# A new order for the operations of a fused attention and MLP kernel

## The chip, the cores and the metric

The kernel runs on one NeuronCore of a Trainium2 chip. The core has five engines that work side by side, each through its own list of instructions and strictly in the order of that list: TensorE (PE, matrix products and the weight loads that precede them), VectorE (DVE), ScalarE (ACT), GpSimd (POOL) and SyncE (SP, which here only issues transfers). An engine that has reached an instruction whose operand is not ready stands still until a semaphore tells it that the operand is there; everything behind that instruction on the same engine stands still too. Transfers between the off-chip memory and the on-chip memory (SBUF) are issued from the lists of SP, ACT and POOL.

The metric is the device time of one launch in microseconds (us). Before the change three runs took 209.41, 209.46 and 210.68 us; the median is 209.46.

## The reference

The reference is attention with a sliding window and a few always visible "sink" keys, followed by a two-layer MLP whose activation is the square of a ReLU:

```python
scores = scale * q @ k.T                      # 4 batches, 8 heads, 768 positions, head width 64
keep = (key < 4) | (0 <= query - key < 128)   # 4 sink keys, a window of 128
a = softmax(where(keep, scores, -1e9))
x = (a @ v), heads side by side               # 3072 tokens x 512
out = relu(x @ w_in) ** 2 @ w_out             # 512 -> 2048 -> 512, float32 out
```

## The kernel before, in words

**Attention.** A batch is 768 tokens: six tiles of 128, taken in three pairs s = 0, 1, 2. For each pair the kernel forms the scores of two heads at a time (the tile `ps`, line 613), turns them into exponentials on ACT (`expm`, line 634), zeroes what lies outside the window (the "mask": on DVE by a product with a triangle of ones, line 646 or 643, or on POOL by two "selects" of line 218), multiplies by the values (`po`, line 682) with a column of ones that gives the softmax's denominator, and divides on DVE (lines 698 and 699, tile `xn`). The result is turned round to put features on partitions: for batches 0 and 1 by PE (`px`, line 731) with a copy out of PSUM, for batches 2 and 3 by transposing transfers issued from SP (line 713, tile `xT`). Queries and keys need the same turning: in the first tiles of batch 0 they arrive in float32 (`qr`), are cast to bf16 (`qs`, the function `regroup`), turned by PE (`pt`, line 507) and copied out of PSUM (`qkT`, the function `unload`); for batches 2 and 3 this too is done by transposing transfers (line 461).

**The MLP.** Layer 1 of batch 0 and of a part of batch 1 is a plain product (`pm`, line 763), then a ReLU and a square. The rest of layer 1 (line 894) and most of layer 2 (line 1233) use Strassen's scheme: seven products in place of eight, paid for by sums and differences on DVE. The sums on DVE are `xs` (line 852, differences of blocks of `xT`), `sg` and a part of `gT` (line 1207, of blocks of the activations), `wi` (lines 810 and 818) and `wt` (line 1025, of blocks of the weights), all of them with two bf16 operands in SBUF; and `t` (line 936) and `r` (line 963), which read PSUM.

**What sets the order.** The function that builds the kernel makes 946 numbered operations, each with the operations it must follow and the memory rooms it takes. An operation is a handful of instructions: the cast of one block, the eight products of one Strassen term, one issue of a transfer. `Plan.run` then emits them one after the other in the order of the string `ORDER`, which is the whole schedule written out by hand or by a search. A word of it is a number, with up to two additions. A letter chooses the engine where an operation can run on several (`55d`: on DVE, `55a`: on ACT, `g`: on POOL). `+0` or `+1` chooses one of two PSUM pools. Rooms of a pool are given out in turn, first freed first used, so that the order also decides which buffer an operation writes and whom it therefore has to wait for:

```python
for s in o.takes:
    if len(s.pools) > 1:
        s.pool = s.pools[int(chosen.pop(0))]
    s.room = free[s.pool].pop(0)
```

Since each engine runs its own list, the order of the string matters in three ways: the order of instructions on each engine, the order of the transfers on the three issuing queues, and the assignment of rooms.

`DUMMIES` gives some operations a number of idle matmuls that are put ahead of their work on PE, to keep the array busy: 29 in operation 945 (`warmup`, line 1363), 8 in 58, 10 in 63, 4 in 64, 3 each in 83, 91 and 97 (line 185).

Operations that the prediction names, all of batch 0: 8 to 15 are the eight transfers of `qr`, in this order on SP; 55, 56, 61, 62, 67, 68, 73, 74 the casts of what they bring; 57, 58, 63, 64, 69, 70, 75, 76 the turns of these on PE; 59, 60, 65, 66, 71, 72, 77, 78 the copies of the turned blocks out of PSUM; 83, 84, 91, 92 the scores of the first pair of tiles, 85, 86, 93, 94 their exponentials on ACT, 87, 89, 95, 97 their products with the values; 103, 104, 113, 114 the scores of the second pair of tiles, 105, 107, 115, 117 their exponentials and 106, 108, 116, 118 their masks; 99 and 101 the turns of the result and 100 and 102 their copies; 156 is the first layer-1 product, with the first quarter of `w_in`, which operation 21 loads. 79 is the preparation of the sink values on POOL.

Of the kernel before, what the change touches and what calls it, by code (L numbers as in the profile page):

```python
# [18 lines left out]


ORDER = """
944 0 1 2 7 8 9 10 11 12 13 14 15 16 17 18 945+0 3 5 19 20 21 6 79 22 23 24 25 55d 56d 57+0 58 59d 60a 83+0 85 103+1
105 26 27 28 62d 61d 63+1 64 67d 68d 65a 69+0 70 71d 72d 66a 84+1 73a 74a 75+1 76 78d 91+0 86 77a 93 80 113+1 87+0
92+1 89 94 95+0 97 115 88 90 96 98 114+1 99+0 101 117 100d 104+0 81+1 102d 107 82 4 29 106g 30 31 32 33 34 35 36 37 38
39 40 41 42 43 44 45 46 127 47 48 49 50 116d 118d 108d 156+0 109+1 119+1 121 111 162+0 110 120 122 112 123+1 125 124d
126d 157a 163a 158a 164a 168+1 165+0 51 52 53 54 177+0 169a 170d 208g 166a 167a 178d 171+1 179a 172a 128+1 131+0 174+0
173a 132a 129d 319 323 321 175d 324 176d 322 130a 320 159+1 133a 160a 161a 278+0 279 136+1 144+0 145+0 280 281 148 138
146 289+1 149d 139d 274 147d 275 282 290 283 291 292 284 276 277 134+1 137+0 135 286a 140 141d 285 287d 293 150+0 151
294 142+1 196+0 192+1 295 143 193 200+1 198a 202a 195d 197 199d 201 203d 297d 194d 296 298a 152+1 154 204+0 205
212+0+1 153a 155d 189+0 215 206a 213 190a 214 207d 186+0 216 191d 248+0 187d 249d 251+1 209 253a 188d 252a 180+1 181d  # L30
250d 182d 183+0 326 184a 185d 300 301 230+0+1 233 299 288 219+0+1 231 220 304+0 210+0 306a 211 222 305 237+0+0 240
232d 325 302 221 303 223 241d 238 239d 311 307 217+1 254+0 224+0 308a 255 309 218 242+0 225 243 452g 422 423 424 425
426 427 428 429 430 431 432 433 434 234g 235+1 226+0 228 310a 227a 229a 314 236 244+0 246 316a 247a 327 313 245d 329
256+0+1 257 315 328 332 317 330 347+1 333+1 348 334 259 335a 337 312 336 331 338 349a 263+1+1 266 264 339 351 340 341a
350 352 435 436 437 258g 438 439 267g 265g 361+0 353 362 354 363d 260g 364 343 365 366 445 440 453 444 441 355a 356a
342a 448 446 449 442 447 443 451 450 318 344 345 357 375+0 358 376 261+0 359 377a 346a 367 368 379 378 262 380 268+0
270+0 381 382 360a 369a 271a 269 370d 371 272 273d 372 383a 389 373 463+0+0 385 386 466 464 390 408+0 409 394+1 395
410a 391 393 387 411 396a 397 412 456+1+0 413 392 414 398 400 415 374d 388a 457 384a 399 504 458 506 465 467 505 508+0
416a 401 418 419 510a 511 402a 654 655 684g 656 657 658 659 660 661 662 663 664 665 672 459 420 460 685 512a 417a 421a
403a 404 468+0 509 405 513 454+1 469 406 507 514a 455 515 461+0 472+1+0 407a 517 523 542 462 518 519 521 544 675 673  # L40
470 473 546+0 475 543 548a 479+0+0 516 520d 549 480 482 550a 524 481d 545 476d 525 483d 547 495+1+0 551 553 496 552a
498 556 674 676 666 667 668 474g 669 670 499g 471 522 679 488+0+0 555 554 526 497d 484+1 557 491 489 671 492g 490g
477+0 500+0 485 478 559 501 561 527+0 528 529d 563 562 493+0 565 558d 494 534 530 535 531d 566+0 567 532 533a 568d 569
564 570 572 571 536 683 682 677 678 486 502 680 711+0+0 487 503 573 574d 537 538 539d 540 681 541 560 714 712 704+0+0
580+0 581 576 577 582d 583 594 584 585 575a 705 707 688+0+0 713g 715g 706g 708g 689 691 578 586 587 626+1 627 588a
628a 612+0 686+0 613 687 630 596 692 690 595 629 631 716+0 717 589a 614a 632 633 579a 634a 635a 615 590 616 597 617
693+0 694 591 618 636 619 637 592 598+1 599 620a 600a 638 593a 601 622 640+0 641 602 623 642a 736 643 603 644 604 646
605 645 709+0 647 624 740+0 639a 621a 606a 648a 742a 649a 607a 608 609 738 737 650 651 743 739 710 610 611d 741
695+0+0 744a 625a 696 698 652 653d 755 697 699 756 757 745 747 746a 749 748 720+0+0 723 759+0 750 700+0 701 761a 762
751 721 752a 763a 760 722g 753 724g 727+0+1 774 775 758 728 730 725+0 766 764 778+1 779 765a 729d 767 776 726 777 768  # L50
731g 732+1 733 718 719 702 703 754 734 735 793 794 785 770 769 798+1 812+0 799 813 780a 771a 800a 814a 781 782a 797
796 786 772 795 815 801 802 816 817 818 803 783 819 784d 787 820a 804 805 789 822 823 829 826 827 828 791 806a 807a
821a 808 809 788 830+0 831 790a 832a 824 825d 810 858+1 811a 834 872+0 844+1 860a 846a 874a 833 835 836 837 873 845
859 876 838a 839a 886 887 888 875 877 861 840 841 848 862 864 792 773 842 863 847 889 849 878 879 890+0 865 843a 880a
850 882 883 851 892a 881a 866d 867d 884 893 894d 868 869 852a 853a 854 855 870 856 895 891 897 896a 885a 900 857d 871d
905 909+1 899 907 901 924 926 906 898 925 903 911a 912 913a 902a 928+1 904 914 910 929 931+1 915d 908 927 918 920 919
930a 933a 916 922 921d 934 917 923 932 935 936 939 937 938 943 940 942 941
"""
DUMMIES = {
    945: 29, 58: 8, 63: 10, 64: 4, 83: 3, 91: 3, 97: 3,  # L60
# [1340 lines left out]
```

## Time and profile before

| | |
|---|---|
| timed runs | 209.41, 209.46, 210.68 us |
| the profiled execution, first to last instruction (span) | 208.3 us |
| TensorE's granted clock, mean over the span | 1.000 |
| PE busy | 200.5 us (96%), 2476 matmuls |
| weight loads busy | 174.3 us (84%) |
| DVE busy | 173.1 us (83%), 318 instructions |
| ACT busy | 135.9 us (65%), 189 instructions |
| POOL busy | 96.4 us (46%), 138 instructions |
| DMA moved | 26.1 MB |

The page gives the span of the profiled execution, 208.3 us; its own time beyond that is not listed, so what lies around the span is taken from the median of the timed runs: 209.46 - 208.3 = 1.16 us. Rows of a timeline read: start in us from the beginning of the span, length in us, engine, line, operation, what is written and read, size, count, and in brackets the idle time of that engine just before and who ended it. Line numbers are those of the kernel before; the changed kernel's are lower by one from the end of `ORDER` on, since the new string is one line shorter.

### The profile page before, as it was taken

What the parts mean: (1) busy time and instruction counts of PE and PEld (TensorE: products, weight loads), DVE (VectorE), ACT (ScalarE), POOL (GpSimd) and SP (SyncE); (2) the same over time, 40 slices, a digit from 0 to 9 for tenths busy, and PEclk for the clock granted to TensorE, in tenths of its full rate; (3) what the DMA queues carried; (4) which work ended last, traced back from release to release, by engine and by line L of the source; (5) the groups of instructions that cost most, each with busy time, mean ns of one, the idle gap of its engine ahead of it and who ended that gap; (6) DMA issues with size and microseconds to landing.
All of it is one profiled execution on the core that took longest, in us unless ns stands there. A gap on an engine that the chain in (4) does not pass through costs nothing.

```text
span 208.3 us, 5924 instructions
## 1 busy us (share of the span) xinstructions
PE 200.5 (96%) x2476; PEld 174.3 (84%) x2476; DVE 173.1 (83%) x318; ACT 135.9 (65%) x189; POOL 96.4 (46%) x138
## 2 busy tenths in 40 slices
PE   7989999999998999999999998999999999999993
PEld 7658997457986889989878987999888999998893
DVE  6759268867599998999999987999989598999933
ACT  2695888433749589999987047988856248693110
POOL 7999274599599976689356209000043000000000
PEclk9999999999999999999999999999999999999999
DMA  6999999999999999999999945300204203200115
GB/s 190 260 184 207 173 196 215 166 146 142 261 68 148 131 172 137 181 162 121 154 116 220 109 96 134 148 3 0 50 14 145 50 5 113 88 3 0 50 54 201
DMA packets 93994, 26.10 MB, mean 125 GB/s; under 512 B 86800, under 2 KB 91408, under 8 KB 93968
## 3 DMA queue, kind: packets, MB, share of 16 engines
q0 software_dynamic: 69248, 12.59, 80.2%
q1 hardware_dynamic: 24536, 13.01, 27.9%
q8 instruction: 19, 0.31, 0.6%
q10 hardware_dynamic: 184, 0.14, 0.2%
q14 instruction: 7, 0.06, 0.1%
HBM read 27.30 MB, written 6.29 MB: 161 GB/s over the span
## 4 chain that ended last, share of the span: by engine, by line
PE 82%; DVE 5%; DMA 4%; SPq 3%; ACT 2%; issue 2%; DVEq 0%; ACTq 0%
PE py L1233 26%; PE pm L894 23%; PE pm L763 10%; PE py L984 7%; PE po L682 6%; PE ps L613 4%; DMA qr<-in_q_dram 3%; PE pt L507 2%; PE py L1094 2%; SPq L351 2%; DVE t L936 1%; PE px L731 1%; DMA xT<-xn_sb 1%; SPq L461 1%; ACT expm L634 1%
## 5 line engine op out<-in xcount | busy, mean ns | idle before, releaser
L634 ACT ACTIVATE expm<-ps 128x1024 bf16<-128x1024 f32 (+1 forms) x48 | 43.7, 953 | 7.7 <-PE ps L613 7.5
L218 POOL TENSOR_SCALAR_AFFINE_SELECT expm<-expm 128x512 bf16<-128x512 bf16 x34 | 22.7, 705 | 44.2 <-ACT expm L634 40.4
L894 PEld LDWEIGHTS <-w_in_sb 128*128 128x128 bf16 x384 | 32.2, 114 | 2.0 <-issue 1.9
L1233 PEld LDWEIGHTS <-gT_sb 128*128 128x128 bf16 x288 | 27.2, 98 | 4.7 <-issue 1.4
L917 ACT ACTIVATE gT_sb<-r 128x1024 bf16<-128x1024 bf16 x28 | 28.8, 1054 | 2.5 <-DVE r L963 2.3
L894 PE MATMUL pm<-xs,wi 128*128 128x256 bf16 (+1 forms) x288 | 29.2, 246 | 0.1
L192 ACT ACTIVATE osb<-py 128x256 f32<-128x256 f32 (+1 forms) x30 | 11.9, 399 | 25.0 <-PE py L1233 19.8
L936 DVE TENSOR_TENSOR t<-t,pm 128x512 f32<-128x512 f32 x36 | 23.8, 683 | 3.7 <-PE pm L894 2.9
L894 PEld LDWEIGHTS <-wi 128*128 128x128 bf16 x288 | 24.6, 114 | 1.0 <-DVE xs L852 0.4
L1233 PEld LDWEIGHTS <-sg 128*128 128x128 bf16 x216 | 20.3, 98 | 2.7 <-issue 0.5
L963 DVE CUSTOM_DVE_ANT_1 r<-pm,t 128x1024 bf16<-128x1024 f32 x18 | 21.8, 1218 | 0.5 <-PE pm L894 0.5
L763 PE MATMUL pm<-xT,w_in_sb 128*128 128x256 bf16 x192 | 22.0, 273 | 0.0
L763 PEld LDWEIGHTS <-w_in_sb 128*128 128x128 bf16 x192 | 20.6, 114 | 0.3 <-issue 0.2
L894 PE MATMUL pm<-xs,w_in_sb 128*128 128x256 bf16 (+1 forms) x192 | 19.9, 246 | 1.0 <-DVE t L936 1.0
L951 ACT ACTIVATE r<-pm 128x1024 bf16<-128x1024 f32 x16 | 16.3, 1022 | 4.9 <-DVE osb L194 2.3
L1233 PE MATMUL py<-w_out_sb,gT_sb 128*128 128x256 bf16 x144 | 18.7, 273 | 0.6 <-ACT expm L634 0.6
L1233 PE MATMUL py<-wt,sg 128*128 128x256 bf16 x144 | 18.7, 273 | 0.0
L1233 PE MATMUL py<-wt,gT_sb 128*128 128x256 bf16 x144 | 18.5, 273 | 0.0
L682 PEld LDWEIGHTS <-expm 128*128 128x128 bf16 x352 | 16.6, 97 | 1.9 <-issue 0.6
L682 PE MATMUL po<-v,expm 128*128 128x65 bf16 x352 | 17.8, 193 | 0.3 <-ACT expm L634 0.3
L699 DVE TENSOR_TENSOR xn_sb<-po,rc 128x512 bf16<-128x512 f32 (+1 forms) x28 | 17.2, 615 | 1.0
L984 PE MATMUL py<-w_out_sb,gT_sb 128*128 128x512 bf16 x64 | 14.8, 379 | 0.0
(104 smaller groups left out, 376.9 us busy)
## 6 DMA issues: line engine op xcount, KB each, us to landing
out_dram<-osb SPq DMA_DIRECT2D x11, 512.0 KB, 3.7
v<-in_v_dram POOLq DMA_DIRECT2D x24, 128.0 KB, 6.2
qn<-in_k_dram POOLq DMA_DIRECT2D x20, 128.0 KB, 6.1
qn<-in_q_dram POOLq DMA_DIRECT2D x20, 128.0 KB, 6.5
w_in_sb<-in_moe_w_in_dram POOLq DMA_DIRECT2D x4, 512.0 KB, 9.4
w_out_sb<-in_moe_w_out_dram POOLq DMA_DIRECT2D x4, 512.0 KB, 10.8
qr<-in_k_dram SPq DMA_DIRECT2D x4, 256.0 KB, 5.1
qr<-in_q_dram SPq DMA_DIRECT2D x4, 256.0 KB, 4.8
```

The source lines that it names most:

```text
L218: nc.gpsimd.affine_select(out=e_tile, in_=e_tile, compare_op=ALU.is_ge, fill=fill, base=i - 1, pattern=[[0, n], [1 if i else -1, 128]], ch ...
L634: nc.scalar.activation(out=x[:, :, o:512], in_=bank_t["s", b, s, m][:, :, o:512], func=AF.Exp, scale=scale)
L682: touch(("po", b, s, m0), e, nc.tensor.matmul(pv[:, i, h2, :], lhsT=lhsT, rhs=rhs, start=(n_ == 0), stop=(n_ == len(mms) - 1)), j)
L699: touch(("po", b, s, m0), e, nc.vector.tensor_tensor(out=xn_sb[:, 2 * s:2 * s + 2, 128 * (m0 + j0):128 * (m0 + j0 + nj)].rearrange("p i (j ...
L763: nc.tensor.matmul(pm[:, i, :], lhsT=w_in_sb[:, fb // 4, kb, fb % 4:512:4], rhs=xT[:, c0 // 256:(c0 + cw) // 256, kb, :], start=(kb == 0), ...
L894: touch(tag, e, nc.tensor.matmul(y[:, bk, i, :], lhsT=weights(name, f0 + i, a), rhs=rhs[:, a, :], start=fresh and i == 0 and a == 0, stop= ...
L917: nc.scalar.activation(out=d, in_=x, func=AF.Square)
L936: touch(tag, e, nc.vector.tensor_tensor(out=T["t"], in0=T["t"], in1=T["y"][:, bk], op=ALU.subtract), bk)
L951: touch(tag, e, nc.scalar.activation(out=r, in_=T["y"], func=AF.Relu), 0, 1)
L963: touch(tag, e, nc.vector._custom_dve(TENSOR_ADD_SAT, out=r.rearrange("p b n c -> p b (n c)"), in0=T["y"].rearrange("p b n c -> p b (n c)" ...
L984: touch((b, u), e, nc.tensor.matmul(pm[:, i, :], lhsT=gT_sb[:, fb, 128 * t:128 * t + 128], rhs=w_out_sb[:, fb, :], start=(fb == 0), stop=( ...
L1233: touch((b, u), e, nc.tensor.matmul(region(name), lhsT=x[:, i, :], rhs=w_[:, i, :], start=first and i == 0, stop=i == HB - 1, skip_group_c ...
```

## The change

Only the string `ORDER` changes. The 946 operations, their instructions' shapes, the idle matmuls and all other code stay as they are. The new string was found by a search over orders in a replay that models the times at which DVE's sums and GpSimd's selects collide. Of the operations 65 are given to another engine than before; the counts that come of it:

| operation | before | after |
|---|---|---|
| masks | DVE 27, POOL 17 | DVE 28, POOL 16 |
| casts of `qr` (`regroup`) | DVE 6, ACT 2 | DVE 4, ACT 2, POOL 2 |
| ReLUs of plain layer 1 and Strassen layer 1 (`relu`) | ACT 24, DVE 6 | ACT 25, DVE 5 |
| squares of plain layer 1 | ACT 6, DVE 6 | ACT 9, DVE 3 |
| copies of turned blocks (`unload`) | ACT 12, DVE 12 | ACT 11, DVE 13 |

The first lines of the string, where operations 1 to 200 stand, and its last line:

```diff
-944 0 1 2 7 8 9 10 11 12 13 14 15 16 17 18 945+0 3 5 19 20 21 6 79 22 23 24 25 55d 56d 57+0 58 59d 60a 83+0 85 103+1
-105 26 27 28 62d 61d 63+1 64 67d 68d 65a 69+0 70 71d 72d 66a 84+1 73a 74a 75+1 76 78d 91+0 86 77a 93 80 113+1 87+0
-92+1 89 94 95+0 97 115 88 90 96 98 114+1 99+0 101 117 100d 104+0 81+1 102d 107 82 4 29 106g 30 31 32 33 34 35 36 37 38
-39 40 41 42 43 44 45 46 127 47 48 49 50 116d 118d 108d 156+0 109+1 119+1 121 111 162+0 110 120 122 112 123+1 125 124d
+8 0 944 5 55a 9 10 1 11 12 13 14 15 7 3 6 57+1 56d 19 2 58 59a 61d 20 67 60a 68d 945+0 63+1 21 62a 22 23 103+1 73d 74
+64 69+0 24 25 83+0 4 71 65a 105 66a 84+1 70 26 85 75+1 79 72a 86 91+0 76 87+0 27 77 78 89 28 92+1 90 93 114+1 95+0 29
+88 94 97 117 96 30 31 99+0 113+1 80 98 100 32 16 33 34 35 36 115 101 81+1 104+0 102 37 38 116d 156+0 39 82 106d 107
+119+1 118d 109+0 121 108d 40 41 110 42 122 111 162+1 112 43 123+0 120 124 125 168+1 126a 44 163 169 45 157d 164a 170a
...
-930a 933a 916 922 921d 934 917 923 932 935 936 939 937 938 943 940 942 941
+920 932 935 934 922 936 939 921d 937 938 923 943 940 942 941
```

What the prediction speaks of, engine by engine:

- **PE, start.** Before: 945 (29 idle matmuls), 57, 58, 83, 103, 63, 64, 69, 70, 84, 75, 76, 91, 113, 87, 92, 89, 95, 97, 114, 99, 101, 104, 81, 156. After: 57, 58, 945, 63, 103, 64, 69, 83, 84, 70, 75, 91, 76, 87, 89, 92, 114, 95, 97, 99, 113, 101, 81, 104, 156. The same operations stand ahead of 156.
- **ACT, start.** Before: the transfer 7, then 60, 85, 105, 65, 66, 73, 74, 86, 77, 93, 80, 94. After: 55, the transfer 7, 59, 60, 62, 65, 105, 66, 85, 72, 86, 93, 94, 117, 80.
- **POOL, start.** The loads keep their order among themselves. Two casts (67, which waits for transfer 12, and 74, which waits for transfer 15) now stand between them: 67 ahead of the first quarter of `w_in` (21), 74 ahead of the second (24). The preparation of the sink values (79) moves behind all four quarters of `w_in`. The selects of operation 106 go to DVE.
- **SP, batch 2.** The four transposing transfers of the last two pairs of `xT` (486, 502, 487, 503) stand one behind the other; before, a transposing transfer of batch 3's keys (680) stood between 502 and 487.
- **The end.** The last four product operations on PE (932, 935, 936, 939) and what follows them are in the same order as before, but that 921 and 923 come later.

61 lines of the change are left out of this document (30 added, 31 removed).

## The prediction

> **What bounds the kernel now.** I read the page first: the span, the engines' shares and the chain of work that ended last.
>
> ```profile
> span 208.3 us, 5924 instructions
> PE 200.5 (96%) x2476; PEld 174.3 (84%) x2476; DVE 173.1 (83%) x318; ACT 135.9 (65%) x189; POOL 96.4 (46%) x138
> PE 82%; DVE 5%; DMA 4%; SPq 3%; ACT 2%; issue 2%; DVEq 0%; ACTq 0%
> ```
>
> TensorE is busy for 96% and is 82% of the chain. An order can only win where PE stands still, so I asked next for busy times by stretches, cut where PE's share falls.
>
> ```profile
> 0.00:17.00 17.00, 14.69 (x180) 11.14 (x181) 11.51 (x32) 11.23 (x17) 15.28 (x30) 1.00 1.24 211
> 17.00:60.00 43.00, 43.00 (x459) 34.27 (x458) 29.40 (x51) 25.57 (x35) 29.19 (x40) 1.00 1.72 177
> 60.00:65.00 5.00, 4.02 (x49) 2.99 (x47) 4.88 (x9) 3.97 (x7) 5.00 (x7) 1.00 2.09 133
> 65.00:120.00 55.00, 54.85 (x797) 48.77 (x795) 52.83 (x102) 44.02 (x62) 37.91 (x50) 1.00 1.85 150
> 120.00:130.00 10.00, 9.03 (x138) 7.80 (x136) 7.64 (x13) 6.61 (x8) 4.94 (x8) 1.00 0.49 108
> 130.00:203.00 73.00, 73.00 (x844) 67.69 (x843) 64.86 (x111) 44.53 (x63) 4.08 (x6) 1.00 0.16 53
> 203.00:208.30 5.30, 1.96 (x26) 1.68 (x24) 1.95 (x5) 0.00 (x0) 0.00 (x0) 0.99 0.55 198
> ```
>
> The second column is the stretch's length, the third PE's busy time. From 17 to 203 us PE is idle for 0.00 + 0.98 + 0.15 + 0.97 + 0.00 = 2.1 us. That is all that an order can win in the middle. DVE's 52.83 of 55 us are close to a bound, but the 0.15 us beside it say that PE hardly waits for it. The end (5.3 us) is the last product, its sums and the last store; its order is kept, so I cost it at nothing. What is left is the start, where PE's share is padded by idle matmuls. The chain of waits shows what set it:
>
> ```profile
> 4.48 6.15 DMA qr<-in_q_dram
> ...
> 10.72 0.64 ACT qs L192
> ...
> 13.76 0.82 ACT expm L634
> ...
> 16.62 1.87 PE pm L763 x16
> ```
>
> The last transfer of `qr` (15) lands at 10.63, a cast takes 0.64, the last exponential of the first tiles (94) runs from 13.76 to 14.58, and the first layer-1 product (156) starts at 16.6. From there to 60 us PE never stops. So the time is the start of 156, plus PE's work (the same operations after 156 in both orders), plus PE's waits, plus the end.
>
> **Term 1, the start.** Timelines of PE and ACT:
>
> ```profile
> 1.27 3.28 PE L1363 MATMUL pw<-tri 128*128 128x128 bf16 x29 [1.27 <-DVE tri L224]
> 4.34 0.63 PE L507 MATMUL pt<-ident,qs 128*128 128x128 bf16 x4
> ...
> 5.62 0.63 PE L507 MATMUL pt<-ident,qs 128*128 128x128 bf16 x4
> ...
> 7.48 0.73 PE L185 MATMUL pt<-ident 128*128 128x128 bf16 x10
> 8.19 0.40 PE L507 MATMUL pt<-ident,qs 128*128 128x128 bf16 x4
> ```
>
> ```profile
> 8.08 1.02 ACT L634 ACTIVATE expm<-ps 128x1024 bf16<-128x1024 f32 x1
> 8.98 1.09 ACT L192 ACTIVATE qkT<-pt 128x512 bf16<-128x512 bf16 x2
> 9.94 1.41 ACT L192 ACTIVATE qs<-qr 128x512 bf16<-128x512 f32 x2
> 11.25 0.79 ACT L634 ACTIVATE expm<-ps 128x768 bf16<-128x768 f32 x1
> ```
>
> The 29 idle matmuls take 3.28 us, the last one alone 0.31, so they start (3.28 - 0.31) / 28 = 0.106 us apart. The ten of 7.48 are (0.73 - 0.22) / 9 = 0.057 apart. PE runs at half rate first and at full rate from about 7 us. The old order puts the 29 where PE has nothing to do, before the first cast is ready. The new one puts them behind the first two turns. There: 55's cast (now ACT, 0.64) ends near 4.2, as DVE's did. Turns 57, eight idle matmuls, turns 58 are 16 x 0.106 = 1.7 us, to 5.9. The 29 at half rate end at 5.9 + 3.1 = 9.0; if the rate doubles at 6.8, at 8.0. Then ten more idle matmuls and the turns of 63, at full rate 0.57 + 0.22: 63 is done, with 0.2 us through the array, near 10.0 in the first case, 9.0 in the second, and 10.75 if the half rate lasts. Before it was done at 8.59, and what it waits for (cast 61) is there by then in every case.
>
> Behind 63 the new order chains ACT, one step after another with rows of 0.55 to 0.60 (copy out), 1.02 (exponential, 1024 wide), 0.8 (768 wide). From 63 at 10.0: copy 65 to 10.65, exponential 105 to 11.6, copy 66 to 12.15, exponential 85 to 12.9, copy 72 (after turn 70) to 13.6, exponential 86 to 14.4, exponential 93 to 15.15; score 92, behind copies on DVE, is ready at 15.7 and exponential 94 ends at 16.5. Before it ended at 14.58. From there to 156 lie a product with values, a division, a turn and a copy in both orders, 16.6 - 14.6 = 2.0 us. So 156 starts at 18.5: **+1.9 us**, between +0.9 (63 done at 9.0) and +2.7 (10.75). In the old order 85 and 105 were done before 65; that cover is what the moved 29 take away. That transfer 15 lands late no longer hides anything: its cast on POOL ends near 11.3, and PE takes it up (76) at 14.
>
> Beside it: the Trainium skill, "TensorE: Matmul & The Clock Gate", section "What's actually happening", says that the array's clock is halved by default and freed after a free-running window of about 3.4 us has been busy. The trace agrees (0.106, then 0.057, with the step after 5.5 us of work). By that rule PE, busy only from 4.2, would be freed between 7.6 and 11.0, and the sum would lie between my middle and upper case, against this change.
>
> The loads of `w_in` must still be there for 156. Rows for them and for a cast on POOL, which no trace shows:
>
> ```profile
> 5.61 0.76 POOL L308 DMA_DIRECT2D w_in_sb<-in_moe_w_in_dram  x1
> ...
> 6.91 2.02 POOL L554 TENSOR_TENSOR vs<-vs_in,head_rows 32x130 bf16<-32x130 f32 x4
> ```
>
> ```profile
> 7.02 2.20 DVE L194 CAST qs<-qr 128x512 bf16<-128x512 f32 x4 [1.28 <-DMA qr<-in_q_dram]
> ```
>
> ```profile
> w_in_sb<-in_moe_w_in_dram POOLq DMA_DIRECT2D x4, 512.0 KB, 9.4
> ```
>
> DVE did the four casts from 7.02 on without another wait, 0.55 each; transfer 12 has landed by about 7.7. POOL's cast lies between 0.55 (DVE's) and 2.02 (the four sink products, 520 elements a partition): I take 0.7, nearer to the same operation. So 21 is issued near 8.4 instead of 5.61 and lands 9.4 later, at 17.8: 0.7 us ahead of 156, cost nothing. At 2.0 it lands at 19.1, and 156 starts 0.6 later. The masks moved from POOL to DVE right after this (106) fall where PE did not wait before: nothing.
>
> **Term 2, the waits in the middle.** The gap before 130 us:
>
> ```profile
> 122.25 2.03 SPq L461 DMA_TRANSPOSE qkT<-qn  x1
> ...
> 124.34 2.57 SPq L713 DMA_TRANSPOSE xT<-xn_sb  x2
> ...
> 128.27 0.95 DVE L852 TENSOR_TENSOR xs<-xT 128x512 bf16<-128x512 bf16 x1 [0.64 <-DMA xT<-xn_sb]
> ...
> 129.14 0.68 DVE L936 TENSOR_TENSOR t<-t,pm 128x512 f32<-128x512 f32 x1
> ...
> 129.87 0.61 PE L894 MATMUL pm<-xs,w_in_sb 128*128 128x128 bf16 x8 [0.97 <-DVE t L936]
> ...
> 130.87 0.41 DVE L852 TENSOR_TENSOR xs<-xT 128x512 bf16<-128x512 bf16 x1
> ```
>
> PE waits 0.97 for a difference `t` behind `xs`, which waits for the transposed `xT` and then takes 0.95 instead of 0.41, because selects run on POOL beside it: the collision that the search is about, 0.54 us. `xT` came late since SP was 2.03 us in the transpose of 680. The new order puts 680 behind all four of `xT`; PE's work between the last values of batch 2 and the first use of this `xs` is 10.8 us in the new order against some 5 us for four issues, 2.5 for the landing and 0.4 for the sum. So this wait goes: **-0.97**.
>
> Beside it: the Trainium skill, "SBUF — State Buffer", section "Who interferes with whom", says that a VectorE instruction with two SBUF operands and a GpSimd one that reads SBUF exclude each other, and that one with a PSUM operand is untouched. The trace agrees (0.95 against 0.41 for `xs`; `t` at 0.68). It would let at most these 0.54 us and none of the other gap depend on collisions.
>
> The gap from 60 to 65 us has another cause:
>
> ```profile
> 61.03 1.02 ACT L775 ACTIVATE r<-pm 128x1024 bf16<-128x1024 f32 x1 [2.63 <-PE pm L763]
> ...
> 61.95 2.64 ACT L634 ACTIVATE expm<-ps 128x1024 bf16<-128x1024 f32 x3
> 62.10 0.34 PE L613 MATMUL ps<-qkT 64*128 64x256 bf16 x4 [0.40 <-ACT r L775]
> ...
> 63.02 1.03 PE L1233 MATMUL py<-w_out_sb,gT_sb 128*128 128x256 bf16 x8 [0.57 <-ACT expm L634]
> ```
>
> PE wants PSUM rooms that ACT has still to empty. In the new order, from the end of the last plain layer-1 product, ACT owes a ReLU, two wide exponentials, a sink exponential (0.4) and two narrow ones, some 4.7 us with their overlap, before PE may go on; PE has 3.4 us of work between (three scores, a sink score, two Strassen terms). That is 1.3 late; the same sum over the old order gives 1.2 where the rows show 0.97. So I keep **1.1**, and the 0.15 elsewhere goes or stays. Waits: 2.1 before, 1.2 after: **-0.9 us**, between -1.8 and, since a schedule with 65 operations on other engines may have waits that sums do not show, +1.0 (one more wait like the longest, twice).
>
> **Sum.** 208.3 + 1.9 - 0.9 = 209.3 us of span. The median of the runs lies 209.46 - 208.3 = 1.16 above the profiled span; with it 210.5 us.
>
> **Rivals.**
> 1. *The 29 are hidden* (faster). The half rate ends early, ACT keeps up, 156 starts at 16.6 as before, and only 0.3 us of waits stay: 209.46 - 1.8 = 207.7. For it: 63's data are the bound if they land later than I think. Against: DVE had all casts from 7.02 on.
> 2. *Cold array and late weights* (slower). Half rate until 63 is done, a POOL cast near 2.0: 156 at 16.6 + 2.7 + 0.6; waits unchanged. 209.46 + 3.3 = 212.8. It decides once 63 is done after about 10.7.
> 3. *ACT in place of DVE* (slower). Squares and copies moved to ACT make it the late helper; two more waits of 0.97 beside the 1.2 that I count: 209.46 + 1.9 - 0.9 + 1.9 = 212.4. For it: ACT's share of 44 us in the 55 from 65 on; against: the new order's sum there is no longer than the old one's.
> 4. *Collisions are only moved.* The waits stay at 2.1: 209.46 + 1.9 = 211.4.
>
> **How the numbers follow.** Forecast 0.35, rival 1 0.15, rival 2 0.22, rival 3 0.13, rival 4 0.15. The range 208.0 to 213.2 takes in the start's lower end with the best middle (209.46 + 0.9 - 1.8 = 208.6), a part of rival 1, and rivals 2 to 4. One per cent, 2.1 us, is about what a measurement of this kernel tells from no change. Faster by more needs the start at no cost and the middle without a wait: 0.06. Slower by more is rivals 2 and 3 and the tails of the others: 0.39. Between: 0.55.
>
> **What would show it.** PE's 29 idle matmuls behind eight turns, from 5.9; the first `pm` of line 762 (the old 763) near 18.5; PE idle 0.2 or less around 130 us later shifted by 2; `xs` at 0.41; a gap of about 1 us near 63, behind ACT. I am wrong if the first `pm` starts within 0.5 us of 16.6, or if PE's waits between it and the end come to more than 3 us.

## The result, and where the time went

The new order takes 217.9 us (four runs, 217.27 to 218.63) against 209.8 us for the old one on the same chip: ratio 1.0368, 95% interval 1.0322 to 1.0413. The forecast was 210.5, with a range up to 213.2. Ratios, here and below, leave out executions over 1.5% above the fastest of the same kernel; where such executions are what the case is about, all four times are given instead. The profiled execution of the new order has a span of 215.9 us, 7.6 more than the old one's 208.3.

First the page of the new order: span, engines, the tenths of PE and of the granted clock in 40 slices, and the chain that ended last.

```profile
span 215.9 us, 5917 instructions
PE 202.2 (94%) x2473; PEld 175.3 (81%) x2476; DVE 170.2 (79%) x316; ACT 137.9 (64%) x190; POOL 97.2 (45%) x138
PE   1999999999999999999999399999999999999993
PEclk9999999999999999999999889999999999999999
PE 80%; DMA 8%; ACT 5%; DVE 3%; SPq 1%; issue 1%; DVEq 0%; ACTq 0%
```

One slice of PE falls to 3 (5.4 us a slice, so near 121 us), the granted clock is lower in this slice and the next, and DMA has twice its old share of the chain (8% for 4%). VectorE's busy time went down (170.2 for 173.1); it does not help.

Busy time of the new order by stretches; columns as in the prediction (length, PE, PEld, DVE, ACT, POOL, granted clock, DMA, GB/s).

```profile
17.00:60.00 43.00, 42.74 (x462) 33.21 (x463) 28.85 (x51) 26.19 (x36) 29.51 (x42) 1.00 1.70 166
60.00:65.00 5.00, 4.64 (x50) 3.90 (x47) 4.20 (x9) 4.96 (x8) 5.00 (x6) 1.00 1.28 82
65.00:118.50 53.50, 52.53 (x752) 46.15 (x753) 51.88 (x96) 43.71 (x62) 41.16 (x52) 1.00 1.93 148
118.50:122.20 3.70, 0.24 (x7) 0.14 (x4) 1.41 (x3) 0.38 (x1) 0.00 (x0) 1.00 1.43 201
122.20:126.00 3.80, 3.80 (x45) 3.02 (x45) 0.64 (x2) 1.53 (x3) 0.00 (x0) 0.55 0.60 99
126.00:210.60 84.60, 84.09 (x994) 77.29 (x993) 73.41 (x131) 51.58 (x70) 8.59 (x13) 1.00 0.24 59
```

Outside of 118.5 to 126 PE is idle for 0.26 + 0.36 + 0.97 + 0.51 = 2.1 us between 17 and 210.6, as much as in the old order. New are 3.46 us in which PE stands still, and 3.8 us behind them at a clock of 0.55, which lose 3.8 x 0.45 = 1.7 us. The start, in PE's timeline:

```profile
6.17 3.30 PE L1362 MATMUL pw<-tri 128*128 128x128 bf16 x29
...
9.97 0.39 PE L506 MATMUL pt<-ident,qs 128*128 128x128 bf16 x4
...
18.53 1.69 PE L762 MATMUL pm<-xT,w_in_sb 128*128 128x256 bf16 x14
```

The first layer-1 product comes 1.9 us later than in the old order (18.53 for 16.6). 1.9 + 3.5 + 1.7 = 7.1 of the 7.6 us; the other half microsecond is not assigned (it lies in PE's busy time from the first product on, 188.4 us for 186.3, of which the clock accounts for 1.7, and not in a wait).

The wait itself, in the new order: PE's list of waits (in total, times, longest), then ACT's and SP's timelines and PE's.

```profile
PE py L1232 <- ACT osb L191: 3.5, 1, 3.5
PE pm L893 <- DVE t L935: 0.5, 1, 0.5
```

```profile
121.70 0.38 ACT L191 ACTIVATE osb<-py 128x256 f32<-128x256 f32 x1 [6.43 <-DMA out_dram<-osb]
```

```profile
98.46 13.69 SPq L460 DMA_TRANSPOSE qkT<-qn  x6
112.25 1.23 SPq L712 DMA_TRANSPOSE xT<-xn_sb  x1
113.57 0.54 SPq L1275 DMA_DIRECT2D out_dram<-osb  x1
```

```profile
122.13 1.83 PE L1232 MATMUL py<-wt,sg 128*128 128x256 bf16 x8 [3.46 <-ACT osb L191]
```

Read from the end: Strassen term 530 on PE waits for the copy 529 on ACT; 529 takes the output room that store 522 (rows of batch 1) has to empty; that store was issued by SP at 113.57, behind six batch-3 turns and the transpose 470, and its room was free at 121.7, 8.1 us later. In the old order SP issued it at 111.21, and 529 (there on DVE) had begun by 117.64 at the latest, without PE's waiting:

```profile
111.21 0.54 SPq L1276 DMA_DIRECT2D out_dram<-osb  x1
```

The eight products of 530 then take 1.83 us in the new order instead of 1.03.

Why did the store come late and land slowly? SP's and GpSimd's queues further back, the new order first (SP's timeline, and GpSimd's list of waits), then the old one (SP's timeline):

```profile
66.06 20.16 SPq L460 DMA_TRANSPOSE qkT<-qn  x9
86.28 0.72 SPq L423 DMA_DIRECT2D vs_in<-in_v_dram  x1
87.10 4.82 SPq L460 DMA_TRANSPOSE qkT<-qn  x3
```

```profile
POOL vs L553 <- DMA vs_in<-in_v_dram: 4.0, 1, 4.0
```

```profile
68.37 17.09 SPq L461 DMA_TRANSPOSE qkT<-qn  x12
```

The old order's twelve turns of batch 2 follow one another and are issued by 85.5. The new order's SP starts earlier and is done at 91.9: it stands from 73.1 to 80.3 in front of turn 448, whose load 434 lands only then (at 74.3 in the old order), with ready turns (443, 447, 446) behind it; and the small load 18 (sink rows of batch 3) stands behind turn 447, so that GpSimd's sink products wait 4.0 us for it, with the loads of batch 3 behind them. What the DMA engines did meanwhile (stretches 85 to 95 and 110 to 123; last but one column), new order, then old:

```profile
85.00:95.00 10.00, 9.57 (x153) 8.85 (x151) 9.85 (x18) 9.90 (x14) 3.82 (x7) 1.00 0.88 128
...
110.00:123.00 13.00, 9.51 (x147) 7.77 (x145) 9.18 (x19) 5.41 (x9) 7.74 (x10) 0.97 1.82 171
```

```profile
85.00:95.00 10.00, 9.85 (x154) 8.88 (x152) 9.92 (x20) 9.67 (x14) 7.99 (x12) 1.00 1.64 156
...
110.00:123.00 13.00, 13.00 (x222) 11.72 (x220) 11.82 (x27) 4.62 (x7) 4.91 (x7) 1.00 0.96 151
```

The column adds up what overlaps on an engine, so it can pass 1. In the new order it is 0.88 instead of 1.64 from 85 to 95, and 1.82 instead of 0.96 from 110 to 123, just when SP's transfers are wanted. So there were two readings to tell apart: the store's place in SP's queue, or a shortage of DMA time that was made 20 to 30 us earlier.

### The profile page after: what moved, and what is told of

It reads as the page before. It is cut to its first block, busy times and chain, and to the rows that moved or that the text cites. A ratio compares the mean times of both kernels' runs of the same rounds, so it can differ in the third digit from the quotient of the medians.

```text
span 215.9 us, 5917 instructions
## 1 busy us (share of the span) xinstructions
PE 202.2 (94%) x2473; PEld 175.3 (81%) x2476; DVE 170.2 (79%) x316; ACT 137.9 (64%) x190; POOL 97.2 (45%) x138
## 4 chain that ended last, share of the span: by engine, by line
PE 80%; DMA 8%; ACT 5%; DVE 3%; SPq 1%; issue 1%; DVEq 0%; ACTq 0%
PE pm L893 23%; PE py L1232 23%; PE pm L762 8%; PE py L983 6%; PE po L681 5%; PE ps L612 5%; DMA out_dram<-osb 4%; PE pt L506 3%; DMA xT<-xn_sb 2%; PE py L1093 2%; PE pw L1362 1%; DMA qr<-in_k_dram 1%; PE px L730 1%; SPq L712 1%; ACT gT_sb L916 1%
## 5 line engine op out<-in xcount | busy, mean ns | idle before, releaser
L893 PE MATMUL pm<-xs,wi 128*128 128x256 bf16 (+1 forms) x288 | 30.1, 246 | 0.4 <-ACT r L950 0.4
L916 ACT ACTIVATE gT_sb<-r 128x1024 bf16<-128x1024 bf16 x27 | 27.7, 1052 | 0.8 <-DVE r L962 0.7
L950 ACT ACTIVATE r<-pm 128x1024 bf16<-128x1024 f32 x18 | 18.4, 1020 | 8.0 <-PE pm L893 4.3
L1232 PE MATMUL py<-wt,sg 128*128 128x256 bf16 x144 | 19.5, 280 | 3.5 <-ACT osb L191 3.5
L681 PE MATMUL po<-v,expm 128*128 128x65 bf16 x352 | 18.6, 196 | 0.3 <-ACT expm L633 0.2
L681 PEld LDWEIGHTS <-expm 128*128 128x128 bf16 x352 | 17.3, 99 | 1.6 <-ACT expm L633 0.4
L1246 DVE TENSOR_TENSOR osb<-py,osb 128x256 f32<-128x256 f32 x27 | 11.1, 419 | 4.9 <-ACT osb L191 2.5
```

The source lines that it names most:

```text
L681: touch(("po", b, s, m0), e, nc.tensor.matmul(pv[:, i, h2, :], lhsT=lhsT, rhs=rhs, start=(n_ == 0), stop=(n_ == len(mms) - 1)), j)
L893: touch(tag, e, nc.tensor.matmul(y[:, bk, i, :], lhsT=weights(name, f0 + i, a), rhs=rhs[:, a, :], start=fresh and i == 0 and a == 0, stop= ...
L916: nc.scalar.activation(out=d, in_=x, func=AF.Square)
L950: touch(tag, e, nc.scalar.activation(out=r, in_=T["y"], func=AF.Relu), 0, 1)
L1232: touch((b, u), e, nc.tensor.matmul(region(name), lhsT=x[:, i, :], rhs=w_[:, i, :], start=first and i == 0, stop=i == HB - 1, skip_group_c ...
```

## Experiments

All runs at a glance. "First product" is the start of the first layer-1 product in the profiled execution, "rest" its span less that; "wait" is PE's longest near 118 us; the clock is the mean granted one. Ratios are against the old order on the same chip; each comes with its 95% interval.

| kernel | ratio | first product | rest | wait | clock |
|---|---|---|---|---|---|
| old order | 1 | 16.59 | 191.7 | none | 1.000 |
| new order | 1.0368 [1.0322, 1.0413] | 18.53 | 197.3 | 3.5 | 0.992 |
| warm_first | 1.0247 [1.0186, 1.0308] | 16.49 | 196.3 | 3.2 | 0.992 |
| sinks_early | 1.0288 [1.0228, 1.0348] | 17.67 | 197.9 | 3.8 | 0.984 |
| store_early | 1.0277 [1.0198, 1.0356] | 17.05 | 197.0 | 3.9 | 0.992 |
| sinks_warm | 1.0233 [1.0159, 1.0307] | 16.63 | 197.6 | 3.6 | 0.984 |
| turns_ready | 1.0095 [1.0061, 1.0128] | 17.79 | 193.4 | 1.8 | 1.000 |
| turns_warm | 1.0028 [0.9997, 1.0059] | 16.46 | 191.9 | 0.7 | 1.000 |
| turns_only | 212.98, 216.34, 216.58, 216.72 us | 17.33 | 197.7 | 4.0 | 0.984 |
| turns_score | 211.50, 215.14, 215.54, 215.77 us | 16.68 | 197.4 | 3.4 | 0.984 |
| gap_filled | 1.0316 [1.0235, 1.0397] | 17.13 | 196.3 | 0.6 | 1.000 |
| other_work_first | 1.0439 [1.0320, 1.0559] | 17.41 | 198.8 | 5.3 | 0.983 |
| loads_held | 1.0231 [1.0131, 1.0331] | 17.66 | 200.5 | 2.7 + 2.8 | 0.984 |
| loads_held_2 | 1.0157 [1.0089, 1.0225] | 17.51 | 195.9 | 0.9 + 2.0 | 0.989 |
| all_repairs | 1.0203 [1.0144, 1.0262] | 16.65 | 196.6 | 2.7 | 0.992 |
| small_v | 1.0051 [1.0013, 1.0088] | 17.36 | 191.1 | none | 1.000 |
| before_late_loads | 1.0127 [1.0092, 1.0162] | 17.35 | 193.5 | none | 1.000 |
| before_680 | 0.9961 [0.9933, 0.9989] | 16.73 | 190.6 | none | 0.997 |

### The start, and two small repairs of the queue

**warm_first**

```diff
-... 944 5 55a ... 60a 68d 945+0 63+1 ...
+... 944 945+0 5 55a ... 60a 68d 63+1 ...
```

> The changed order with the 29 idle matmuls (945) at the front again, as in the order before; nothing else. Theory S (the start is a delay of its own): 63 is done near 8.6 instead of 10.0, the chain on ACT behind it starts 1.4 earlier, the first layer-1 product comes at 17.0 instead of 18.53: 216.4 (215.9 to 217.0). Rival: the middle hangs on transfers, not on PE, so PE only waits longer there: 217.5 to 217.9 with a wait of 5 us instead of 3.5 near 118.

The first product comes at 16.49, earlier than the 17.0 expected, and the wait stays (3.2 for 3.5): the start is a delay of its own, and the transfers moved along with it. Ratio 1.0247 for 1.0368, and the intervals do not overlap. The table tells something more: the ten kernels with the 29 idle matmuls behind the first turns have their first product between 17.05 and 18.53 (mean 17.5), the five new orders with them in front between 16.46 and 16.68 (mean 16.6). So the usual price of that move is 0.9 to 1.0 us; the 1.9 of the profiled execution is its upper end. (The two changed old orders further down, also with them in front, have 16.73 and 17.35; the second stood 1.1 us for a cast on ACT.)

**sinks_early**

```diff
-SP: ... 17 299 442 441 440 444 445 448 443 449 447 18 450 451 446 ...
+SP: ... 17 18 299 442 441 440 444 445 448 443 449 447 450 451 446 ...
```

> The changed order with one word moved: load 18 (the sink rows of batch 3, on SP) stands right behind load 17 instead of behind the batch-2 turns 443, 449 and 447. Base 217.9 us. Theory L (late loads): GpSimd's sink products 684 stood 4.0 us for this load, its loads of batch 3 left about 4 us later, the backlog of loads made SP's transfers take 8 us, and the store 522 freed its room at 121.7. Then the 3.5 us of PE's wait and the half-rate stretch behind it (about 1.9) go: 212.5 to 213. Theory Q (only the place of store 522 on SP, behind the turns 676 and 679 and the transpose 470): nothing changes for it, 217.9, at best 217.

GpSimd no longer waits for the sink rows, but then for other things: 2.0 us for PE's values of batch 1 and 3.9 us for a turn that has to free a room. The loads of batch 3 leave about as late as before (the first three at 88.9, 89.8 and 94.6, for 91.0, 92.0 and 94.9), and the wait stays at 3.8. Load 18 alone is not the cause; this half of theory L fell.

**store_early**

```diff
-SP: ... 675 676 679 470 522 471 677 ...
+SP: ... 675 676 522 470 679 471 677 ...
```

> The changed order with store 522 right behind the last sum that it needs (516), and the turn 679 and the transpose 470 behind it. Theory Q: issued at 110.5 instead of 113.57, it lands 3.1 us earlier, at 118.6; PE's wait falls from 3.5 to 0.5 us and the half rate does not come: 213. Theory L: the store is issued earlier but every transfer of SP still takes 8 us beside the late loads, so the next wait is the transposed xT of 471 (landing near 122.5): PE still waits 1.5 to 2 us, 215.5 to 216.5.

The store is issued at 109.11 and ACT's copy 529 runs at 116.81, at no cost to PE. But PE waits, now for the scores 711:

```profile
PE ps L611 <- DMA qkT<-qn: 3.9, 1, 3.9
```

Every transfer of SP is late, and the store was only the first that PE asked for. Its place on SP is not the cause, either.

**sinks_warm**: load 18 and the idle matmuls both moved.

> Both: load 18 behind 17, and the 29 idle matmuls at the front. Theories L and S together: 217.9 - 5.2 - 1.5 = 211.2 (210.2 to 212). If only the place of store 522 counts (Q): 216.4. If the start is swallowed by transfers: as sinks_early alone.

It comes out as warm_first does (1.0233 and 1.0247): nothing is gained by load 18 there.

### The turn that stood at the head of SP's queue

**turns_ready**

```diff
-SP: ... 17 299 442 441 440 444 445 448 443 449 447 18 450 451 446 ...
+SP: ... 17 18 299 442 441 440 444 445 443 447 446 448 449 450 451 ...
```

> The changed order; on SP the batch-2 turns 443, 447 and 446, whose loads land by 79.8, stand ahead of turn 448, which waits till 80.28 for load 434, and load 18 stands behind 17. Theory T (the cause sits earlier: SP stood 7.2 us, from 73.1 to 80.3, in front of turn 448 while ready turns stood behind it; so the turns of batch 2 end at 91.9 instead of 85.5, their rooms come free late, the loads of batch 3 leave 4 to 5 us late, and every transfer of SP between 98 and 123 lands 8 us after its issue): the turns end near 86, the loads of batch 3 and store 522 land 4 us earlier, PE's wait at 118 falls from 3.5 to at most 0.5 us, the granted clock stays 1.00, and of the 217.9 us some 6 go: 211.5 to 212.5. Theory Q (the place of the store among its neighbours on SP): 217.5 or more. Half way: the wait only gets shorter, the clock still falls: 215 to 217.

**turns_warm**: the same, with the idle matmuls in front.

> The same with the 29 idle matmuls at the front again. Theory T with the start's 1.9 us: 209.6 to 210.6, within 0.5% of the order before. If the wait at 118 stays: 215.7 as with the idle matmuls alone.

With four words of SP moved, 2.7% go, and with the start as well the new order is within 0.6% of the old one. SP is done with batch 2 at 87.6 and 85.5 (91.9 before); the DMA engines are less idle from 85 to 95, 1.55 and 1.68; PE's wait is 1.8 and 0.7, and the clock stays at 1.000. The rows of turns_warm:

```profile
63.62 21.86 SPq L459 DMA_TRANSPOSE qkT<-qn  x12
85.59 0.52 SPq L1274 DMA_DIRECT2D out_dram<-osb  x1
```

```profile
85.00:95.00 10.00, 9.58 (x153) 8.75 (x150) 9.58 (x19) 9.89 (x14) 9.34 (x14) 1.00 1.68 212
```

**turns_only**: the three turns moved, load 18 left where it was. **turns_score**: turns_warm, and 677 and 678 ahead of 470.

> The changed order; only the turns 443, 447 and 446 stand ahead of 448 on SP, load 18 stays behind turn 449. It tells apart the two edits of the earlier run that had both (ratio 1.0095). If SP's stand in front of turn 448 is the cause by itself: 1.008 to 1.012, PE's wait near 118 below 2 us, clock 1.00. If load 18 is needed as well: 1.02 or more, with GpSimd's sink products waiting some 2 us or more for it.

> The changed order with all three repairs (turns 443, 447, 446 ahead of 448; load 18 early; the idle matmuls at the front), and the turns 677 and 678 ahead of the transpose 470. The 0.7 us that PE still waited for the score 711 near 118 should go: 0.3% less than without this edit (1.0028), 0.999 to 1.001. If the transposes behind them come late instead: 1.003 or more.

The gain did not hold in either; turns_only came out as the second case of its expectation has it (load 18 is needed as well). One execution of each is near the repaired order that it was made from (212.98 us, 211.50 us, clock 1.000), the profiled ones show the wait again, 4.0 and 3.4 us, and the other two of each have their times and a clock of 0.984 to 0.990. In the profiled turns_only GpSimd waited 5.4 us for load 18, so that load counts beside the turns, though moving it alone did not help. turns_score has no such reason, and its DMA engines were at 1.66 from 85 to 95, as busy as those of turns_warm: the wait near 118 does not need engines that stood idle there. What tips its executions is not settled. The repaired orders stand close to the edge (turns_ready too has one execution in ten at 216.56 and 0.984), while none of the 62 executions of the old order measured beside these kernels lies above 212.8.

### What the standing still costs

**gap_filled**

```diff
 DUMMIES = {
-    945: 29, 58: 8, 63: 10, 64: 4, 83: 3, 91: 3, 97: 3,
+    945: 29, 58: 8, 63: 10, 64: 4, 83: 3, 91: 3, 97: 3, 530: 58,
 }
...
         def product(n, name, lhs, rhs, first, after, follow=(), takes=(), reads=()):
             def run(e):
...
+                if P.idle:
+                    warm(region("d")[:, 0:128], (b, u), 1)
                 for i in range(HB):
```

> The changed order; PE runs 58 idle matmuls (128x128, 57 ns apart, 3.3 us) in the wait for store 522's room, ahead of the Strassen term 530. Theory H (the array falls to half rate because it stood still): the clock stays 1.00, the wait itself stays, and the 1.7 us (clock 0.992) to 3.5 us (0.984) that the runs of the changed order lose go: 215 to 215.5 (span 213 to 214.2). Rival: the lower rate comes from what runs there and not from the idle time: clock 0.984 to 0.992 as before, 217.9.

```profile
117.58 3.40 PE L183 MATMUL py<-ident 128*128 128x128 bf16 x58
121.63 1.03 PE L1233 MATMUL py<-wt,sg 128*128 128x256 bf16 x8 [0.64 <-ACT osb L190]
```

The wait for the store is as long as before, but PE works on nothing meanwhile, the clock is 1.000 in all four executions, and the products of 530 take 1.03 us. So the rate falls because PE stands still. What it is worth in time this run does not settle: its four executions lie between 215.16 and 218.22, since the landing of the store itself varies; by the clocks of the new order's own four executions (0.992, 0.990, 0.984, 0.984 of 216 us) it is 1.7 to 3.5 us.

**other_work_first**

```diff
-PE: ... 527 500 530 493 711 528 566 ...
+PE: ... 527 500 493 711 528 530 566 ...
```

> The changed order; on PE the Strassen term 530, which waits for the room of store 522, stands behind the values 493, the scores 711 and the term 528 (2.3 us of work) instead of ahead of them. In the order before 528, 493 and 534 stand between 527 and 530. If the price comes from what PE has to do meanwhile: its wait falls from 3.5 to about 1.2 us (with up to 0.9 more at the next product, for xT), the clock stays 1.00, and the time is 213 to 214.5. If the granted clock falls for another reason than PE's standing still, 0.984 to 0.992 stay and it is 215.5 or more.

It is no faster than the new order itself (its four executions took 217.90 to 222.01 us). 530 would now have found its room free, but PE came 5.3 us too early to the scores 711, whose turns land near 123:

```profile
PE ps L611 <- DMA qkT<-qn: 5.3, 1, 5.3
```

In the new order these turns were hidden behind the wait for the store. The idea that PE had other work ready was wrong, and the clock (0.983) fell with this longer wait, too.

### Is it DMA time?

**loads_held**

```diff
-POOL: ... 664 665 666 667 668 669 670 476 481 499 492 497 ...
+POOL: ... 664 665 476 481 499 492 666 667 668 669 670 497 ...
-SP:   ... 677 678 681 486 502 487 503 682 ...
+SP:   ... 677 678 486 502 487 503 681 682 ...
```

> The changed order; the last five loads in a row of batch 3 (666 to 670) stand on GpSimd's queue behind the selects, so that they leave after 117 instead of from 102.7 on, and turn 681, which needs 667, stands behind the transposes of xT. Theory D (the store's 8 us are its share of the DMA engines beside the backlog of loads; in the order before one load was open beside it): store 522 lands 4 to 5 us after its issue at 113.6, PE's wait is 0.5 us or less, the clock 1.00: 211.5 to 212.5, unless the held loads are late for the scores of 704 on. Theory P (the place on SP decides, whatever the loads do): 8 us as before, 217.9.

The store was issued at 114.35 and its room was free at 119.06, 4.7 us later instead of 8.1. ACT's row for the copy 529:

```profile
119.06 0.38 ACT L190 ACTIVATE osb<-py 128x256 f32<-128x256 f32 x1 [4.66 <-DMA out_dram<-osb]
```

So over 3 of the 8 us are the loads beside it. The time is another matter (214.89 to 219.90 us, the profiled execution being the longest): the five loads stood ahead of select 497, which made the values late by 2.7 us, and then the turns for 711 by 2.8. The first is a fault of this edit.

**loads_held_2**: the five loads behind 497.

> As the earlier run with the five loads held, but now behind GpSimd's last select of that stretch (497), ahead of which they had stood and which they made 2.7 us late for PE. Theory D: store 522 again lands in 4.5 to 5 us, no wait for it or for select 497; what the scores 711 need (turns 677 and 678, issued near 116) lands before 122: a wait of 1 us at most, clock 1.00: 212 to 213.5. If the transposes of SP need their 8 us whatever stands beside them: 711 waits 2.5 us as it did there, and the time stays at 215 or more.

The store takes 5.1 us (112.76 to 117.90), the select is in time, and 711 still waits 2.0 us: the turns before it now share the engines with the held loads. Ratio 1.0157; the clock fell in one of the four executions. Moving DMA work within the full stretch moves the wait, it does not end it.

**all_repairs**: turns_warm with other_work_first and the loads held as in loads_held.

> All together: turns 443, 447, 446 ahead of 448; load 18 early; idle matmuls at the front; 530 behind other work; the five loads held. The waits left are the 1.5 us of small ones that every run of the changed order shows: ratio 0.994 to 1.000 (209.0 to 210.2). If the wait for the store is still there in some executions, these lie near 214.

It has the fault of loads_held (PE waits 2.7 us for select 497) and loses what turns_warm had.

**small_v**

```diff
+                n = 8 if b == 3 else 128
                 return [nc.gpsimd.dma_start(
-                    out=v_sb[b % 2][:, t, :, 0:D],
-                    in_=v[b, :, 128 * t:128 * t + 128, :].rearrange("h p d -> p h d"))]
+                    out=v_sb[b % 2][0:n, t, :, 0:D],
+                    in_=v[b, :, 128 * t:128 * t + n, :].rearrange("h p d -> p h d"))]
```

> The changed order, word for word; each of the six loads of v of batch 3 brings only 8 of its 128 rows (the rest of the work is done on what lies in the room, so batch 3's output is another one). It takes about 120/128 of 6 x 1.7 us of the DMA engines' time out of the stretch before 123 us (1.7 us: the software queue's 79.3% of 215.9 us over 96 loads), some 9.6 us, and leaves every queue's order as it is. Theory D (the DMA engines are the scarce thing between 60 and 123 us, and PE waits for whichever of SP's transfers it needs first): store 522 lands within 5 us of its issue, the wait near 118 is 0.3 us or less, the clock 1.00, and the start's 1.9 us are all that stays: 211.5 to 212.5. Theory P (the place of the store on SP behind the turns): the store is issued near 113 as before and PE waits 2 us or more: 215 to 218.

This kernel leaves out 120 of every 128 rows of batch 3's values, so it does not compute the reference's output; it serves only to take DMA work away. Its whole list of PE's waits, with the start in the first line:

```profile
PE pt L506 <- ACT qs L190: 4.3, 1, 4.3
PE pm L893 <- ACT r L950: 0.4, 1, 0.4
PE py L1232 <- DVE gT_sb L1206: 0.4, 1, 0.4
PE ps L612 <- ACT r L774: 0.3, 1, 0.3
PE po L681 <- ACT expm L633: 0.2, 1, 0.2
```

No word of the order is changed, SP's queue is the same, and the wait is gone; ratio 1.0051, the start's price and little else. This is the shortage of DMA time, and theory P falls. The engines' column is 0.95 from 85 to 95, nearly as low as in the new order (0.88), and 0.99 from 110 to 123: what went is the load on them later. One thing in the expectation is not shown: the store was issued at 109.46 because the turns ahead of it got their loads earlier, and how long it took, PE's next need (ACT's copy at 116.60) does not tell.

**before_late_loads**, the other way round, in the old order:

```diff
-POOL: ... 433 434 234g 435 436 437 258g 438 439 ...
+POOL: ... 433 234g 258g 434 435 436 437 438 439 ...
```

> The order before, with the loads 434 to 437 of batch 2 moved on GpSimd's queue behind the selects that stand after them (behind word 258), so that 434 leaves near 75.5 and lands near 81 instead of 74.3; nothing else. Theory T, the other way round: SP stands in front of turn 448 till 81, the turns of batch 2 end near 92 instead of 85.5, the loads of batch 3 come late, and PE waits some 3 us near 116 with the granted clock below 1.00 behind it: ratio 1.015 to 1.025 (212.5 to 215). Rival: what follows in that order has room for it: 1.00 to 1.005.

SP is now done with batch 2 at 91.1, about as late as in the new order, yet near 118 us PE does not wait. Of the 1.8 us more in the rest 1.2 are selects that came late behind the moved loads near 84, and 0.5 is a wait for a turn of batch 2 at 91. So late turns of batch 2 do not by themselves make the 3.5 us. The old order has more room there (between 527 and 530 stand 528, 493 and 534 on PE, in the new one only 500); that this is what saves it was not tried. The trace has another difference: the backlog was smaller when SP issued store 522.

That is what the profiled executions have in common, by the times at which GpSimd's loads were issued and landed. Where PE waited 3 us or more near 118, six loads (seven in store_early) were still open when SP issued the store, and the last of them landed between 120.9 and 123.3. In turns_ready there were five (wait 1.8), in turns_warm four, the last landing at 114.7 (wait 0.7), in small_v three (no wait), in before_late_loads one, and in the old order none. What builds the backlog is not shown: with the turns and load 18 moved it was smaller in turns_ready and turns_warm, but not in turns_score.

### The one wait that the prediction meant to go

**before_680**

```diff
-SP: ... 677 678 486 502 680 487 503 681 ...
+SP: ... 677 678 486 502 487 503 680 681 ...
```

> The order before with one word moved: turn 680 behind the four transposes of xT (486, 502, 487, 503), as in the changed order. Step of the prediction (term 2): the wait of 0.97 us at 128.7 goes: ratio 0.995, span 207.3. Rival: turn 680 now ends later and another wait takes its place: no change, span 208.3.

SP's and DVE's timelines of this kernel:

```profile
119.54 5.86 SPq L712 DMA_TRANSPOSE xT<-xn_sb  x4
125.50 2.52 SPq L460 DMA_TRANSPOSE qkT<-qn  x2
```

```profile
127.67 0.49 DVE L851 TENSOR_TENSOR xs<-xT 128x512 bf16<-128x512 bf16 x1
128.08 0.68 DVE L935 TENSOR_TENSOR t<-t,pm 128x512 f32<-128x512 f32 x1
```

The four transposes of `xT` now follow one another, `xs` takes 0.49 us instead of 0.95, and PE's 0.97 us are gone from its list of waits. Ratio 0.9961, interval 0.9933 to 0.9989: this one word makes the only kernel here that is faster than both orders.

## The prediction, point by point

**Term 1, the start (+1.9 us, 156 at 18.5).** 18.53 in the profile; 63's turns ran from 9.97 to 10.36 (forecast done near 10.0), the exponential 94 let PE go on at 16.64 (forecast done at 16.5), and GpSimd's cast took 0.61 (0.7). The mechanism was right; the size was partly luck. Over ten kernels with this start the mean is 17.5, 0.9 to 1.0 us late, which is the lower end that the prediction gave for a half rate that ends early. Rivals 1 and 2 both stayed out: 16.6 was not seen with this start, and 63 was done by 10.4. The 7.6 given as the earliest moment for the full rate with this start was too late: the granted clock rose at 9.56 here, but at 6.83 in store_early, where PE had begun at 4.14.

**Term 2, the waits in the middle (-0.9 us).** This is the step that failed: 5.6 us more in the rest instead of 0.9 less. The waits that it named behaved nearly as forecast once transfers were in time. before_680 shows the -0.97 by itself (span 207.3 for 208.3), and small_v, the new order with DMA time to spare, has a rest of 191.1 against the old order's 191.7, so -0.6 (one profiled execution each). In the new order itself the wait before the second `t` did not go but shrank to 0.50, behind an `xs` of 0.84 where 0.41 was forecast. The gap near 63 was forecast at 1.1 and is 0.27 + 0.07 + 0.13 + 0.40 = 0.9, in four pieces between 63.2 and 66.6 (the last, 0.40, behind VectorE's `gT` and not behind ACT).

What was left out: the list of what turn 680 was moved past was followed to the arrival of `xT`, but not the other words of SP's queue. Store 522 went behind the batch-3 turns, and with it a room that 529 and 530 wait for; load 434 comes later on GpSimd's queue, while turn 448, which needs it, still stands ahead of others on SP; load 18 went from SP's first words to behind turn 447. Each was in the diff. And the DMA engines were taken as free. The old order's page said otherwise (tenths of the DMA engines, and the queue of GpSimd's loads with its share of sixteen engines' time):

```profile
DMA  6999999999999999999999945300204203200115
q0 software_dynamic: 69248, 12.59, 80.2%
```

They are at 9 up to 119 us. The sum asked only when a transfer was issued, not what stood beside it. The range's upper end for this term, "one more wait like the longest, twice", was taken from waits of 1 us; the wait that came was 3.5, since nothing holds a wait for a transfer to the size of those for an engine.

**The clock.** No term stood for a second fall of PE's clock. The prediction used the half rate at the start and did not ask what a new wait would do to it; 1.7 to 3.5 us per execution come from there.

**Rivals.** Rival 3 (ACT late) is not what happened, although ACT is the releaser that PE's list names: ACT had stood 6.43 us for the store itself. Rival 4 (collisions only moved) is right as far as it goes and has little price: VectorE's sums took less time in two groups (`sg<-gT_sb` and `sg<-sg,gT_sb`, 9 each, went from 722 and 718 ns on average to 686 and 695) and more in the three widest `xs` (683 to 787), while the triangle masks on VectorE went from 758 to 773 ns and the selects from 705 to 741; that PE waited for them shows only in the old order's 0.97 us, which before_680 removes, and the new order's 0.50. What the search gained on VectorE was, for the rest, not on the path.

**What would have shown it.** The conditions named were right: PE's waits between the first product and the end came to 5.6 us, over the 3 that were given as the sign of a wrong forecast.

**What stays open.** What tips executions of one kernel between a wait of under 2 us and one of over 3 (turns_only, turns_score); how DMA time is shared between a store, the turns and the loads, of which only the sum was seen; what built the larger backlog, since engines that stood idle from 85 to 95 are found without the wait (small_v) and the wait without them (turns_score); and the half microsecond of the 7.6 that no row explains.

## What to carry to other kernels

When an order is changed, go through the words of every DMA queue one by one, and ask of each what stands ahead of it now, when that becomes ready, and whose room it frees: here a turn whose load is late, at the head of SP's queue, together with a small load behind it, cost more than everything that the engines gained. Where the DMA engines are full, a backlog of loads is paid where it meets the first urgent transfer, and taking the wait away at one place brings out the next transfer. A wait of PE of some 3 us cost half as much again or more here, because the clock fell behind it.

## What the runs showed of the hardware

PE's clock falls after a short stand. Over the profiled executions, by the longest waits near 118 us: 0.7 and 1.8 us, clock 1.000; 0.9 and 2.0 us with 1.8 us of work between them, 0.989; 2.7 us, 0.992; 3.2 to 5.3 us, 0.983 to 0.992; 3.4 us filled with idle matmuls and 0.6 left, 1.000. In loads_held, with two waits of 2.7 and 2.8 us, the clock fell twice (0.984). Behind such a wait the granted clock is 0.50 for 3.41 us (in the new order from 122.20 to 125.61) or for twice that (in sinks_early from 120.60 to 127.42), which costs 1.7 or 3.4 us where PE has work. The 0.997 of before_680 is another thing, a fall at its very end, from 206.06.

The Trainium skill, "TensorE: Matmul & The Clock Gate", section "What's actually happening", has the array go back to half rate after at least one idle window of about 3.4 us, free-running. The stretches' length agrees; but in all_repairs and loads_held_2 the clock fell after 2.7 us and after 2.9 us in two pieces, less than such a window, so the window need not be wholly idle.

How idle it must be, the busy times of single stretches of 3.41 us show roughly. The clock fell behind 1.36 us of work in loads_held_2 (120.09 to 123.50) and behind 1.66 in other_work_first (116.57 to 119.98); it stayed behind 2.12 and 2.63 in turns_ready (117.34 to 120.75 and on to 124.16), and near the end of all_repairs behind 1.45 (208.49 to 211.90), so the bound is not sharp. The rise needs no fully busy stretch either: in store_early it came behind 2.69 us of work (3.42 to 6.83), while 2.58 us in turns_score, after the fall, did not bring it (119.17 to 122.59; the rate rose at 126.00).

The same words at the start give a first product anywhere from 17.05 to 18.53, as the idle matmuls end between 8.09 and 9.47: the moment at which the rate doubles differs from one execution to the next. With the idle matmuls in front the five new orders lie within 0.22 us. The granted clock of the views is 1.00 at the start all the same, though matmuls are 0.106 us apart there: its records begin only with the rise (at 6.8 us in the old order's profiled execution, 9.6 in the new one's), so the means leave the first half rate out.

A 512-KB store on SP took 8.1 us beside a backlog of GpSimd's loads and 4.7 and 5.1 us without most of it; the median of those whose landing the new order's profile has is 3.0 us.
